# Two attention heads at a time: each product with v in one piece, three score buffers of two banks and two single banks, and a new hand-written order

## The chip, the cores and the metric

The kernel runs on one core of a Trainium2 chip. The metric is the device time of one execution in microseconds (us).

## What is computed

Four batches of eight heads attend over 576 tokens with 64 features per head. A score more than tau below its row's maximum is dropped before the softmax. The result goes through a top-2 mixture of eight experts and then through a dense two-layer network.

```python
scores = scale * np.matmul(q, k.transpose(0, 1, 3, 2))          # q, k, v: (4, 8, 576, 64)
thresh = np.max(scores, axis=-1, keepdims=True) - tau
scores = np.where(scores >= thresh, scores, -1000000000.0)
scores = scores - np.max(scores, axis=-1, keepdims=True)
attn = np.exp(scores)
attn = attn / (np.sum(attn, axis=-1, keepdims=True) + 1e-09)
x = np.matmul(attn, v)                                          # then to (2304, 512)
...
for e in range(8):                                              # two experts for each token
    h = np.maximum(x[mask] @ w1[e], 0.0)
    out[mask] += top2_w[mask, k, None] * (h @ w2[e])
...
g = np.where(h > 0.0, h, np.exp(np.minimum(h, 0.0)) - 1.0)      # h = x @ w_in
return g @ w_out
```

## The kernel before

The change lies in the attention, the first 300 us or so. The experts and the dense network behind it are the same code in both kernels.

Heads are taken in 16 pairs. The 2 x 576 queries of a pair make nine units: eight of 128 queries of one head (1 to 8), and unit 0, which holds the last 64 queries of both heads. A unit goes through these steps, which the order names by a letter, a unit and, behind the point, how many pairs it lags behind the newest one:

- `S` (`scores`, L247): four matmuls of 288 columns (eight for unit 0) into two banks of PSUM, a "wide" buffer.
- `R` (`rowmax`, L256), `H` (`thresh`, L260): VectorE reads the buffer for the row maximum and makes the threshold.
- `E` (`expo`, L265): ScalarE reads the buffer and writes the exponentials to SBUF.
- `M` (`mask`, L281): VectorE reads the buffer again, compares with the threshold, multiplies with the exponentials and writes P and its row sums. With that the wide buffer is free.
- `T` (`trans`, L169): four transpositions of P on TensorE into one bank, a "narrow" buffer; `A` (`evac_trans`, L312 and L315): ScalarE copies them to SBUF (`pt`), and the bank is free.

For each half of a pair's queries (half 0 has units 0 to 4, that is 320 columns, half 1 has units 5 to 8, 256 columns) follow `t` and `a` (the last 64 keys' part is transposed and copied to `ptt`, L328 and L332), `p` and `q` (the product with v, L352, and its copy to `ot`, L354), and `f` and `g` (`fin`, L378 and L382: the output is multiplied with a matrix that turns it to token rows and adds the gate's logits; ScalarE copies it to `ftmp`, L404, and GpSimd scales it, L403). Each of `T`, `t`, `p` and `f` needs a narrow bank: 15 of them for a pair.

A product with v has 64 output rows for each of the two heads, so it uses half of TensorE's columns for each head (128x64 in the profile's rows). It is in float32, which the profile shows as two MATMULs for one product: four blocks of 128 keys for two heads are 16 MATMULs, and the last keys (`ptt`) 4 more. Before, each product comes in two parts, `pa` (two blocks) and `pb` (two blocks and the last keys), with other work between, and holds its bank throughout.

PSUM has eight banks. Before, two wide buffers take four and four narrow ones the rest; in the first cycle a third wide buffer stands in for two of the narrow ones.

TensorE, ScalarE and VectorE run in exactly the order in which the code emits: `FIRST`, then `CYCLE` for each pair, then `REST`. GpSimd and the DMA queues are ordered by the framework. `G` and `F` in the order advance the routing of finished tokens to experts, a generator (`gate`), by one step; it comes at two places of the attention, late in it. `X` in `REST` prepares the first expert.

Of the kernel before, what the change touches and what calls it, by code (L numbers as in the profile page):

```python
# [9 lines left out]
F32 = mybir.dt.float32  # L10
# [15 lines left out]
def fused_kernel(ctx, tc, q, k, v, tau, w_gate, noise, wm, wf, out):  # L26
# [4 lines left out]
    NB = S // 128  # L31
# [90 lines left out]
    wide = [psum.tile([128, 2, 512], F32, name=f"bank{i}", bufs=1) for i in (2, 4)]  # L122
    fstack = ExitStack()
    third = fstack.enter_context(tc.tile_pool(name="fill", bufs=1, space=PSUM)).tile([128, 2, 512], F32, name="bank6")
    wide.append(third)

    def filled():

        wide[:] = [x for x in wide if x is not third]
        fstack.close()  # L130
        more = astack.enter_context(tc.tile_pool(name="bpsum", bufs=1, space=PSUM, reuse_waits="tile"))
        narrow[:0] = [more.tile([128, 512], F32, name=f"bank{i}", bufs=1) for i in (6, 7)]
# [184 lines left out]
    def tails(P, half):  # L317

        ps = mi(512)
# [6 lines left out]
        def out():  # L326
            t = PTT[P, half] = apool.tile([128, CW[half]], F32, name=f"ptt{half}", bufs=1)
# [9 lines left out]
    def pv(P, ch, part):  # L337

        vr, vt = VS[P]
        if P not in OT:  # L340
            OT[P] = apool.tile([128, S], F32, name="ot")
        n = CW[ch]
        if part == "a":
            PV_[P, ch] = mi(512)
        ps = PV_[P, ch][:, :n]
        for kb in (range(2) if part == "a" else range(2, NB + 1)):
# [7 lines left out]
        return lambda: act.activation(OT[P][:, o:o + n], ps, AF.Copy)  # L354

    PV_ = {}
# [8 lines left out]
    def fin(P, half):  # L365
# [8 lines left out]
        ps = mi(512)  # L374
# [13 lines left out]
        def post():  # L388
# [6 lines left out]
            if not half:  # L395
                x = tmp[:, 4 * NX:n].rearrange("p (i n) -> p i n", i=1)
                r = slice(b % 2 * 64, b % 2 * 64 + 64)
                for z in range(2):
                    f = slice(z * 64, z * 64 + 64)
                    todo += [(XT[b // 2][r, 2 * j + z:2 * j + z + 1], x[f, :, :D], rinv[f, 2 * NB:]),  # L400
                             (lgh[r, tt:tt + 1, :, 2 * j + z], x[f, :, D:], rinv[f, 2 * NB:])]
            for o, x, ri in todo:
                pool.tensor_tensor(o, x, ri[(slice(None),) * len(ri.shape) + (None,)].to_broadcast(list(x.shape)), op=OP.mult)  # L403
        return lambda: act.activation(tmp[:, :n], ps[:, :n], AF.Copy), post  # L404
# [162 lines left out]
    pool.memset(PTB[0][:, S:], 0.0)  # L567
    dve.memset(wx, 0.0)
# [4 lines left out]
    for s in range(2):  # L573
# [19 lines left out]
        S3.0 S4.0 S8.0 R3.0 E3.0 H3.0 M3.0 R4.0 R8.0 E4.0 H4.0 M4.0 S2.0 H8.0 S1.0 T3.0 E8.0 R2.0 M8.0 E2.0 A3.0 R1.0  # L593
        T4.0 S5.0 H2.0 A4.0 H1.0 E1.0 M2.0 R5.0 H5.0 M1.0 T2.0 E5.0 A2.0 S6.0 R6.0 T1.0 M5.0 S0.0 A1.0 E6.0 R0.0 T5.0
# [658 lines left out]
```

## Time and profile before

| | |
|---|---|
| median of 3 runs | 1210.14 us (1208.78 to 1210.71) |
| the profiled execution | 1208.14 us, of which its span is 1206.3 us |
| TensorE busy | 1165.9 us (97%) |
| VectorE busy | 717.5 us (59%) |
| ScalarE busy | 591.4 us (49%) |
| GpSimd busy | 275.6 us (23%) |
| share of TensorE in the chain that ended last | 87% |
| mean granted clock of TensorE | 0.991 |
| first matmul of the experts | 307.58 us after the span's start |

The span runs from the first to the last instruction; 1.84 us lie around it. "Busy" is the time in which an engine had an instruction under way. For TensorE the profile keeps two rows: PE for the matmuls, whose ends are modelled, and PEld for the loads of their stationary operands, which run ahead of the matmuls; so start-to-start times are the ones to add up.

### The profile page before, as it was taken

The numbers are of one execution on the slowest core, as the hardware profiler recorded it, in microseconds if no ns is written. First come the engines' busy times: TensorE is split into PE (matmuls) and PEld (weight loads), VectorE is DVE, ScalarE is ACT, GpSimd is POOL, SyncE is SP. The second block draws the span as 40 slices with busy tenths as digits, with TensorE's granted clock in tenths as the row PEclk, the third lists the DMA queues.
The fourth block names the chain that finished last, engine by engine and source line by source line (L and its number), as shares of the span: only waits on it lengthen the run. The fifth ranks groups of instructions, "written<-read, shape, count | busy, mean of one in ns | idle before, by whom it ended". The sixth has DMA issues, their size and how long they took to land.

```text
span 1206.3 us, 20167 instructions
## 1 busy us (share of the span) xinstructions
PE 1165.9 (97%) x7488; PEld 1012.3 (84%) x7488; DVE 717.5 (59%) x1560; ACT 591.4 (49%) x1201; POOL 275.6 (23%) x425
## 2 busy tenths in 40 slices
PE   5999999999899999999999999999999999999997
PEld 4777776776689999998999989788999999999996
DVE  6888889888756875656565657274333333333332
ACT  4777777777443433333333332175555444444443
POOL 6544465855520110000000102220111000000000
PEclk8999999999999999999999999899999999999999
DMA  7877765661596775555555435361122011010000
GB/s 203 245 199 228 215 183 142 204 176 71 176 343 218 246 236 167 187 158 202 158 180 157 166 128 170 123 254 52 53 88 71 10 62 53 2 52 19 1 18 20
DMA packets 66057, 169.96 MB, mean 141 GB/s; under 512 B 11424, under 2 KB 11552, under 8 KB 60320
## 3 DMA queue, kind: packets, MB, share of 16 engines
q1 hardware_dynamic: 54784, 138.94, 37.2%
q0 software_dynamic: 5760, 18.88, 4.6%
q10 hardware_dynamic: 5408, 10.78, 2.6%
q8 instruction: 61, 1.00, 0.3%
q14 instruction: 44, 0.36, 0.1%
HBM read 98.21 MB, written 43.52 MB: 117 GB/s over the span
## 4 chain that ended last, share of the span: by engine, by line
PE 87%; DVE 6%; DMA 3%; issue 2%; ACT 1%; POOL 1%; SPq 0%; ACTq 0%; DVEq 0%; POOLq 0%
PE h L834 17%; PE y L850 17%; PE h L1024 17%; PE o L1043 17%; PE bank L247 7%; PE bank L352 6%; PE bank L169 3%; DVE nmax L256 2%; PE h L169 1%; DMA wf_d<-c 1%; DVE P L281 1%; PE bank L378 1%; DMA w<-in_moe_dram 1%; DMA yg<-ys_d,yslot 1%; ACT e L265 0%
## 5 line engine op out<-in xcount | busy, mean ns | idle before, releaser
L1032 DVE SCALAR_TENSOR_TENSOR g<-fr,h 128x256 f32<-128x256 f32 x144 | 60.4, 420 | 172.5 <-ACT fr L1031 172.4
L265 ACT ACTIVATE e<-bank,nmax 128x576 f32<-128x576 f32 x144 | 105.8, 742 | 71.5 <-DVE nmax L256 66.6
L837 ACT ACTIVATE hh<-h 128x320 fp32r<-128x320 f32 (+2 forms) x128 | 55.4, 433 | 151.8 <-PE h L834 148.4
L818 POOL TENSOR_TENSOR c<-c,c 128x512 int32<-128x512 int32 x32 | 41.5, 1296 | 366.0 <-DVE c L817 366.0
L247 PE MATMUL bank<-kT,qT 128*128 128x288 f32 x320 | 105.3, 345 | 20.4 <-DVE P L281 10.3
L256 DVE TENSOR_REDUCE nmax<-bank 128x1 f32<-128x576 f32 x144 | 106.9, 750 | 26.0 <-PE bank L247 20.2
L1030 ACT ACTIVATE fr<-h 128x256 f32<-128x256 f32 x144 | 54.9, 381 | 119.5 <-PE h L1024 119.5
L281 DVE SCALAR_TENSOR_TENSOR P<-bank,thr,e 128x576 f32<-128x576 f32 x128 | 101.1, 815 | 13.1 <-ACT e L265 10.0
L247 PEld LDWEIGHTS bank<-kT,qT 128*128 128x128 f32 x320 | 62.2, 194 | 50.5 <-DVE P L281 31.2
L1034 DVE TENSOR_TENSOR gl<-g,gh 128x256 fp32r<-128x256 f32 x144 | 61.0, 426 | 67.3 <-ACT gh L1033 64.9
L747 POOL DMA_INDIRECT yg<-ys_d,yslot x36 | 38.5, 1071 | 267.9 <-PE h L169 169.4
L838 DVE SCALAR_TENSOR_TENSOR hl<-h,hh 128x320 fp32r<-128x320 f32 (+2 forms) x128 | 62.4, 487 | 61.5 <-ACT hh L837 61.0
L247 PE MATMUL bank<-kT,qL 128*128 128x288 f32 x320 | 92.0, 303 | 0.6 <-DVE qL L204 0.6
L1033 ACT ACTIVATE gh<-g 128x256 fp32r<-128x256 f32 x144 | 59.8, 416 | 62.5 <-DVE g L1032 62.5
L352 PE MATMUL bank<-pt,vr 128*64 128x256 f32 (+1 forms) x512 | 76.4, 419 | 0.0
L312 ACT ACTIVATE pt<-bank 128x512 f32<-128x512 f32 x128 | 71.4, 599 | 4.2 <-PE bank L169 3.6
L169 PE MATMUL bank<-ident,P_r 128*128 128x128 f32 x576 | 63.1, 247 | 3.1 <-DVE P L281 2.3
L169 PEld LDWEIGHTS bank<-ident,P_r 128*128 128x128 f32 x576 | 58.2, 142 | 9.1 <-issue 6.2
L247 PEld LDWEIGHTS bank<-kT,qL 128*128 128x128 f32 x320 | 62.9, 197 | 0.9 <-DVE qL L204 0.9
L1031 ACT ACTIVATE fr<-fr 128x256 f32<-128x256 f32 x144 | 59.9, 417 | 4.0
L352 PEld LDWEIGHTS bank<-pt,vr 128*64 128x64 f32 x512 | 31.8, 136 | 20.1 <-issue 3.6
L834 PE MATMUL h<-xh,w20h 128*128 128x320 f32 (+2 forms) x120 | 38.9, 324 | 0.0
(358 smaller groups left out, 3556.7 us busy)
## 6 DMA issues: line engine op xcount, KB each, us to landing
w<-in_moe_dram SPq DMA_DIRECT2D x36, 1024.0 KB
cr<-in_ffn_dram SPq DMA_DIRECT2D x32, 512.0 KB
xs_d<-t ACTq DMA_DIRECT2D x8, 1280.0 KB
ys_d<-y SPq DMA_DIRECT2D x40, 256.0 KB
xr<-xs_d SPq DMA_DIRECT2D x38, 256.0 KB
qT<-qh SPq DMA_DIRECT2D x60, 144.0 KB
wf_d<-c SPq DMA_DIRECT2D x32, 256.0 KB
w<-wf_d SPq DMA_DIRECT2D x8, 1024.0 KB
```

Of the source, the lines that this page charges most:

```text
L169: pe.matmul(o.bitcast(dt), x.bitcast(dt), ident.bitcast(dt), is_transpose=True, **{"start": True, "stop": True, **kw})
L247: pe.matmul(ps[:, hv, :S // 2], x[:, qc:qc + 128], kx[:, kc:kc + S // 2], start=(m == 0), stop=(m == n - 1))
L256: dve.tensor_reduce(ST[g][0], view(g), axis=AX.XY, op=OP.max, negate=True)
L265: act.activation(e, view(g), AF.Exp, bias=ST[g][0])
L281: dve.scalar_tensor_tensor(o.rearrange("p (a c) -> p a c", a=2), view(g), ST[g][1], E_.pop(g), op0=OP.is_ge, op1=OP.mult, accum_out=SU[P][ ...
L312: act.activation(turned_p(P, s, i // 2)[:, :, c:c + 128], ps, AF.Copy)
L352: pe.matmul(ps[s * 64:s * 64 + 64], lhs, rhs, start=(kb == 0), stop=(kb == NB))
L834: pe.matmul(ps[:, :step], w[:, c, f * 128:(f + 1) * 128], x[:, c, o:o + step], start=(m == 0), stop=(m == 3 * NC1 - 1))
L838: dve.scalar_tensor_tensor(hl[:, o:o + step], ps[:, :step], 0.0, f32(hh[:, o:o + step]), op0=OP.max, op1=OP.subtract)
L850: pe.matmul(Y[t], h[:, t * 128:(t + 1) * 128], w[:, f], start=(first and m == 0), stop=(last and m == 2))
L1024: pe.matmul(ps, w[:, c, f * 128:(f + 1) * 128], x[:, c], start=(m == 0), stop=(m == 3 * NC1 - 1))
L1043: pe.matmul(O[i], h[:, i * 128:(i + 1) * 128], w[:, f], start=(un == f == m == 0), stop=(un == NU2 - 1 and f == UF - 1 and m == 2))
```

## The change

- Each product with v is one step `p` of 16 + 4 MATMULs; a half's bank is held for that stretch alone.
- In `fin` the last 64 tokens of the two heads were two products of 64 output rows each, on half of the columns each. Now each of the two is a product over 128 tokens on all columns, 80 wide, into places of its own beside each other; of each, half of the rows is used. For that `ot` is wider by 64 columns of zeros and has two fixed buffers.
- Three wide buffers and two narrow ones throughout. `mi` no longer takes the narrow buffers in turn but the next one that nobody holds (`taken`).
- A new order. Half 0's product with v and both `fin` steps now lag two pairs behind, so the first cycle of `CYCLE` has none of them and `REST` has them for two pairs. The extra list `SECOND` goes.

```diff
-    wide = [psum.tile([128, 2, 512], F32, name=f"bank{i}", bufs=1) for i in (2, 4)]
...
-        narrow[:0] = [more.tile([128, 512], F32, name=f"bank{i}", bufs=1) for i in (6, 7)]
+    wide = [psum.tile([128, 2, 512], F32, name=f"bank{i}", bufs=1) for i in (2, 4, 6)]
...
-    def mi(*sh):
-        x = slot_of(narrow)[:, :math.prod(sh)]
+    taken = {}
+
+    def mi(key, *sh):
+
+        x = next(x for x in narrow if not any(x is y for y in taken.values()))
+        narrow[:] = [y for y in narrow if y is not x] + [x]
+        if key:
+            taken[key] = x
+        x = x[:, :math.prod(sh)]
...
-    def pv(P, ch, part):
+    def pv(P, ch):
...
-            OT[P] = apool.tile([128, S], F32, name="ot")
+            OT[P] = OTS[P % 2]
         n = CW[ch]
-        if part == "a":
-            PV_[P, ch] = mi(512)
-        ps = PV_[P, ch][:, :n]
-        for kb in (range(2) if part == "a" else range(2, NB + 1)):
+        ps = mi(("p", P, ch), 512)[:, :n]
+        for kb in range(NB + 1):
...
-            for s in range(2):
-                pe.matmul(ps[s * 64:s * 64 + 64, n:n + NX], OT[P][:, MAIN:S], wx[:, j, s], start=True, stop=True)
-            n += NX
+            for s, c in enumerate((MAIN, MAIN - 64)):
+                pe.matmul(ps[:, n:n + NX], OT[P][:, c:c + 128], wx[:, j, s], start=True, stop=True)
+                n += NX
...
-        E7.1 E8.1 H8.1 a0.1 M7.1 G.0 S1.0 M8.1 W.1 T6.1 G.0 R1.0 S2.0 R2.0 H1.0 G.0 H2.0 g1.2 E1.0 E2.0 T5.1 G.0 p0b.1
...
+        T0.1 M6.1 M5.1 S3.0 S1.0 G.0 A0.1 R8.1 E8.1 R3.0 G.0 T1.1 p0.2 H8.1 A1.1 G.0 R1.0 H1.0 E3.0 M8.1 G.0 H3.0 E1.0
+        F.0 t0.1 W.2 S4.0 G.0 q0.2 M3.0 T2.1 a0.1 G.0 R4.0 T5.1 S0.0 A2.1 G.0 A5.1 M1.0 H4.0 R0.0 G.0 t1.1 E4.0 T6.1
...
```

In the middle of the attention TensorE's order is the following, before, from the second MATMUL pair of a first part of half 1 (L352; 64x256 is what one product writes) over a score product (L247) and two transpositions (L169) to the end of the second part:

```order
L352 MATMUL bank_323<-pt_488,vr 64x256
L247 MATMUL bank_144<-kT,qT_156 128x288
L247 MATMUL bank_144<-kT,qL_158 128x288
L247 MATMUL bank_144<-kT,qT_156 128x288
L247 MATMUL bank_144<-kT,qL_158 128x288
L169 MATMUL bank_324<-ident,P_r 128x128 x4
L169 MATMUL bank_142<-ident,P_r 128x128 x4
L352 MATMUL bank_323<-pt_364,vr 64x256
L352 MATMUL bank_323<-pt_488,vr 64x256
L352 MATMUL bank_323<-pt_364,vr 64x256
L352 MATMUL bank_323<-pt_488,vr 64x256
L352 MATMUL bank_323<-ptt_478,vt_161 64x256 x2
```

And after the change, for the same half of the same pair (L348 is the line of the product with v now), with the transpositions ahead of and behind it:

```order
L165 MATMUL bank_141<-ident,P_r 128x128 x4
L348 MATMUL bank_142<-pt_455,vr 64x256
L348 MATMUL bank_142<-pt_322,vr 64x256
L348 MATMUL bank_142<-pt_455,vr 64x256
L348 MATMUL bank_142<-pt_322,vr 64x256
L348 MATMUL bank_142<-pt_455,vr 64x256
L348 MATMUL bank_142<-pt_322,vr 64x256
L348 MATMUL bank_142<-pt_455,vr 64x256
L348 MATMUL bank_142<-pt_322,vr 64x256
L348 MATMUL bank_142<-ptt_475,vt_158 64x256 x2
L165 MATMUL bank_141<-ident,P_r 128x128 x4
```

The score product and the two transpositions between the parts stand elsewhere in the cycle, and the two banks 141 and 142 take turns between transpositions and product.

Around `fin` of half 0 TensorE has before (transpositions into three narrow banks, then `fin`, L378 and L382, then the score product that takes the buffer 143):

```order
L169 MATMUL bank_324<-ident,P_r 128x128 x2
L169 MATMUL bank_142<-ident,P_r 128x128 x4
L169 MATMUL bank_141<-ident,P_r 128x128 x4
L378 MATMUL bank_323<-wx,ot 128x160 x2
L382 MATMUL bank_323<-wx,ot 64x80 x2
L247 MATMUL bank_143<-kT,qT_151 128x288
L247 MATMUL bank_143<-kT,qL_153 128x288
L247 MATMUL bank_143<-kT,qT_151 128x288
L247 MATMUL bank_143<-kT,qL_153 128x288
```

After, with both `fin` steps (L377, and L381 in place of L382) behind one another:

```order
L243 MATMUL bank_144<-kT,qT_148 128x288
L243 MATMUL bank_144<-kT,qL_150 128x288
L243 MATMUL bank_144<-kT,qT_148 128x288
L243 MATMUL bank_144<-kT,qL_150 128x288
L377 MATMUL bank_142<-wx,ot_167 128x160 x2
L377 MATMUL bank_141<-wx,ot_167 128x160 x2
L381 MATMUL bank_141<-wx,ot_167 128x80 x2
L165 MATMUL bank_142<-ident,P_r 128x128 x4
```

The last tokens' products have 128 rows in place of 64, a score product stands ahead of the two `fin` steps, and a transposition behind them.

ScalarE's order shows how the narrow banks come free. Before, around the copy of a half's product (L354; L312 and L315 copy transpositions, L265 is an exponential, L404 copies `fin`):

```order
L265 ACTIVATE e<-bank_143,nmax 128x576
L265 ACTIVATE e<-bank_144,nmax 128x576
L312 ACTIVATE pt_1179<-bank_324 128x4x128
L312 ACTIVATE pt_1179<-bank_142 128x4x128
L354 ACTIVATE ot<-bank_323 128x320
L265 ACTIVATE e<-bank_143,nmax 128x576
L265 ACTIVATE e<-bank_144,nmax 128x576
L328 ACTIVATE ptt_1206<-bank_141 128x256
L312 ACTIVATE pt_1216<-bank_323 128x4x128
```

After, around the copy of half 0's product (L353), where the copies L326, L330 and L309 empty the banks of the steps `t`, `T2` and `T5` in turn (L261 is an exponential):

```order
L353 ACTIVATE ot_167<-bank_142 128x320
L326 ACTIVATE ptt_1135<-bank_141 128x256
L330 ACTIVATE ptt_1135<-bank_141 64x64 x2
L309 ACTIVATE pt_1070<-bank_142 128x4x128
L309 ACTIVATE pt_1155<-bank_141 128x4x128
L261 ACTIVATE e<-bank_145,nmax 128x576
```

Before, a copy is followed by others from three more narrow banks; now bank 141 and bank 142 alternate, and each copy stands between TensorE's steps of one before and one after.

## Rows read from the trace of the kernel before

**Rows 1.** Page, part 4: the chain that ended last, by engine

```profile
PE 87%; DVE 6%; DMA 3%; issue 2%; ACT 1%; POOL 1%; SPq 0%; ACTq 0%; DVEq 0%; POOLq 0%
```

**Rows 2.** Timeline of TensorE, first `fin` products of L382: first, tenth and last cycle

```profile
36.98 0.36 PE L382 MATMUL bank<-wx,ot 128*64 128x80 f32 x4
...
193.25 0.36 PE L382 MATMUL bank<-wx,ot 128*64 128x80 f32 x4
...
303.27 0.36 PE L382 MATMUL bank<-wx,ot 128*64 128x80 f32 x4
```

**Rows 3.** Busy time by stretch: length, each engine busy, granted clock, DMA

```profile
54.32:71.67 17.35, 17.11 (x135) 13.06 (x135) 15.07 (x39) 13.45 (x28) 9.33 (x19) 1.00 0.78 221
...
195.00:212.00 17.00, 15.40 (x125) 11.34 (x125) 15.80 (x64) 11.85 (x26) 10.21 (x26) 1.00 0.50 127
```

**Rows 4.** Waits from 20 to 300 us: total, times, longest

```profile
PEld bank L247 <- DVE P L281: 29.6, 55, 1.6
...
DVE nmax L256 <- PE bank L247: 18.8, 52, 2.2
...
ACT e L265 <- DVE nmax L256: 59.5, 90, 3.1
```

**Rows 5.** Timeline, half 1's product in two parts; start, duration

```profile
109.70 1.08 PE L352 MATMUL bank<-pt,vr 128*64 128x256 f32 x8
...
110.72 0.40 PE L247 MATMUL bank<-kT,qT 128*128 128x288 f32 x1
...
112.09 1.08 PE L352 MATMUL bank<-pt,vr 128*64 128x256 f32 x8
...
113.01 0.60 PE L352 MATMUL bank<-ptt,vt 128*64 128x256 f32 x4
...
113.54 0.40 PE L247 MATMUL bank<-kT,qT 128*128 128x288 f32 x1
```

**Rows 6.** Timeline of the last pair, where both parts follow one another

```profile
303.46 2.04 PE L352 MATMUL bank<-pt,vr 128*64 128x256 f32 x16
...
305.19 0.75 PE L352 MATMUL bank<-ptt,vt 128*64 128x256 f32 x4
...
305.86 0.88 PE L169 MATMUL bank<-ident,t 128*128 128x128 f32 x8
```

**Rows 7.** Timeline around `fin` of half 0

```profile
105.69 0.78 PE L378 MATMUL bank<-wx,ot 128*128 128x160 f32 x4
...
106.39 0.20 PEld L382 LDWEIGHTS bank<-wx,ot 128*64 128x64 f32 x4 [0.17 <-issue]
...
106.97 0.40 PE L247 MATMUL bank<-kT,qT 128*128 128x288 f32 x1 [0.22 <-DVE P L281]
...
107.34 0.29 PE L247 MATMUL bank<-kT,qT 128*128 128x288 f32 x1
```

**Rows 8.** Timeline, one transposition and ScalarE's copies out of narrow banks

```profile
113.05 0.59 ACT L312 ACTIVATE pt<-bank 128x512 f32<-128x512 f32 x1
...
114.17 0.46 PE L169 MATMUL bank<-ident,PT_r 128*128 128x128 f32 x4
...
116.76 0.38 ACT L328 ACTIVATE ptt<-bank 128x256 f32<-128x256 f32 x1
...
117.02 0.44 ACT L332 ACTIVATE ptt<-bank 64x64 f32<-64x64 f32 x2
...
121.49 0.45 ACT L354 ACTIVATE ot<-bank 128x320 f32<-128x320 f32 x1
```

**Rows 9.** Timeline, start of the second and of the last cycle, and the experts

```profile
47.83 0.40 PE L247 MATMUL bank<-kT,qT 128*128 128x288 f32 x1
...
298.49 0.87 PE L169 MATMUL bank<-ident,P_r 128*128 128x128 f32 x8
...
308.41 3.01 PE L834 MATMUL h<-xb 128*128 128x256 f32 x23 [0.45 <-DVE xb L695]
```

**Rows 10.** Timeline, TensorE's longest wait in the first expert

```profile
320.19 0.73 PE L850 MATMUL y<-w01h,hl 128*128 128x512 f32 x1 [3.91 <-DVE hl L838]
```

More of the change, by code (lines that the diff above doesn't have):

```diff
@@ L121, in fused_kernel @@
     narrow = [psum.tile([128, 512], F32, name=f"bank{i}", bufs=1) for i in range(2)]
-    wide = [psum.tile([128, 2, 512], F32, name=f"bank{i}", bufs=1) for i in (2, 4)]
[L123 to L131, printed above, removed]
-        narrow[:0] = [more.tile([128, 512], F32, name=f"bank{i}", bufs=1) for i in (6, 7)]
+    wide = [psum.tile([128, 2, 512], F32, name=f"bank{i}", bufs=1) for i in (2, 4, 6)]
     def slot_of(slots):
@@ L308, in evac_trans @@
         ps = PS_.pop(g)
+        taken.pop(("T", g))
         if u:
@@ L317, in tails @@
     def tails(P, half):
-        ps = mi(512)
+        ps = mi(("t", P, half), 512)
         for n in range(2):
@@ L326, in out @@
         def out():
+            taken.pop(("t", P, half))
             t = PTT[P, half] = apool.tile([128, CW[half]], F32, name=f"ptt{half}", bufs=1)
@@ L353, in pv, with out @@
         o = OC[ch]
-        return lambda: act.activation(OT[P][:, o:o + n], ps, AF.Copy)
-    PV_ = {}
+        def out():
+            taken.pop(("p", P, ch))
+            act.activation(OT[P][:, o:o + n], ps, AF.Copy)
+        return out
     G2, NX = 2 * E, D + 2 * E
@@ L373, in fin @@
                 XT[b // 2] = xpool.tile([128, H, D], F32, name="xt", bufs=2)
-        ps = mi(512)
+        ps = mi(("f", P, half), 512)
         n = 4 * NX
@@ L399, in post, with out @@
                     f = slice(z * 64, z * 64 + 64)
[L400 to L401 removed]
+                    todo += [(XT[b // 2][r, 2 * j + z:2 * j + z + 1], x[f, z:z + 1, :D], rinv[f, 2 * NB:]),
+                             (lgh[r, tt:tt + 1, :, 2 * j + z], x[f, z:z + 1, D:], rinv[f, 2 * NB:])]
             for o, x, ri in todo:
                 pool.tensor_tensor(o, x, ri[(slice(None),) * len(ri.shape) + (None,)].to_broadcast(list(x.shape)), op=OP.mult)
[L404 removed]
+        def out():
+            taken.pop(("f", P, half))
+            act.activation(tmp[:, :n], ps[:, :n], AF.Copy)
+        return out, post
     SC, SCN = [], set()
@@ L567, in fused_kernel @@
     pool.memset(PTB[0][:, S:], 0.0)
+    OTS = [apool.tile([128, S + 64], F32, name=f"ot{i}", bufs=1) for i in range(2)]
+    for t in OTS:
+        pool.memset(t[:, S:], 0.0)
     dve.memset(wx, 0.0)
@@ L614, in run @@
         elif x == "p":
-            AFTER["p" + g[0], P] = pv(P, int(g[0]), g[1])
+            AFTER[what, P] = pv(P, int(g))
         elif x == "f":
@@ L704, in fused_kernel @@
             u = 0
-            for x in REST if c == NP else SECOND + CYCLE if c == 1 else CYCLE if c else FIRST:
+            for x in REST if c == NP else CYCLE if c else FIRST:
                 what, lag = x.split(".")
@@ L718, in fused_kernel @@
                     next(first, 0)
-                if c == 0 and what == "S6":
-                    filled()
                 if what[0] == ("p" if c == NP and u else "M"):
```

30 lines of the change are left out of this document (14 added, 16 removed).

## The prediction

> **What bounds the kernel now.** I read the page first: TensorE makes 87% of the chain that ended last [rows 1]. So the question is where TensorE's time in the attention goes, since nothing else is edited. The timeline of TensorE gives the beat: the `fin` product of L382 comes once in a cycle, at 36.98 in the first and at 193.25 nine cycles later, which is 17.36 us for one, and at 303.27 in the last [rows 2]. The last six take 110.02 us in place of 104.2: 5.9 us more, in the cycles in which the routing's steps run beside the attention.
>
> The table by stretch shows what a cycle is made of: TensorE 17.11 of 17.35 us, VectorE 15.07, ScalarE 13.45 [rows 3]. TensorE is the bound, with VectorE 13% behind. The list of waits says how TensorE and VectorE are tied: its loads of `kT` and `qT` waited 55 times, 29.6 us in all, for a mask (L281), that is for a wide buffer to come free, some 3.5 times in a cycle for 0.54 us. VectorE waited 52 times for score products, and ScalarE 90 times for a row maximum, 59.5 us in all [rows 4]. These are the waits of a loop through two wide buffers: a buffer is filled, reduced, exponentiated, masked, and only then filled again.
>
> **The change part by part, for one cycle.**
>
> *(a) Each product in one piece.* Half 1's product takes 1.02 us for its first part (109.70 to 110.72) and 1.45 for its second (112.09 to 113.54), 2.47 together [rows 5]. In the last pair the two parts already stand behind one another: 16 MATMULs take 1.73 us (303.46 to 305.19) and the last four 0.67 up to the next transposition [rows 6], or 0.53 up to a score product [rows 5]: 2.40 or 2.26. So one piece saves 0.07 to 0.21 us. A transposition follows it now, but I do not know how much of the 0.67 is that; I take 0.15, and as much for half 0, since what is saved is a second entry and exit and not columns: 0.3, bounds 0.14 and 0.42.
>
> *(b) The last tokens' products over all columns.* Four MATMULs of 160 columns on the whole array take 0.70 us (105.69 to 106.39). Those of L382, 80 wide on half of the columns, take 0.58, of which 0.22 are a wait for a mask: 0.36 [rows 7]. Four of 80 columns on the whole array are half of 0.70, 0.35: nothing lost. The Trainium skill speaks against this edit: by "TensorE: Matmul & The Clock Gate", Part 3, products in different column tiles run at the same time, so putting two such products on the whole array makes them follow one another. By that rule the 0.36 would double, 5.8 us more over 16 pairs; the row of 160 columns says otherwise, and I go by the row. What the edit and the new place of `fin` can give is the 0.22 wait at the score product behind it, since a transposition stands there now and the mask has a third buffer's time: 0.2, bounds 0 and 0.22.
>
> *(c) Three wide buffers.* A matmul whose load could not run ahead shows 0.40 us, the ones behind it 0.29 [rows 7]. With a third buffer the mask that frees a buffer lies a whole unit of VectorE's work further back (15.07 us for nine units, 1.7 us [rows 3]), so loads can run ahead again. Of the 3.5 such waits in a cycle one is counted in (b); 2.5 times 0.11 are 0.25, bounds 0 and 0.4.
>
> *(d) Two narrow banks in place of four.* This is the price. All 15 fills of a cycle now alternate between two banks, so a fill starts only when ScalarE has emptied the one before the last. A transposition has its result after 0.46 us, and the copy takes 0.59 [rows 8]: 1.05 us in which one bank is bound, while TensorE makes something of about that length between two uses of a bank almost everywhere (a score product is 0.63, 113.54 to 114.17 [rows 5, 8]; a product with v over 2). The tightest place that I find is behind half 0's product. There TensorE goes on with `t`, `S4` and `T2`, 0.63 and twice 0.3 to 0.46, 1.2 to 1.5 us, and then wants for `T5` the bank of `t`. ScalarE must first copy the product (0.45) and then the two pieces of `ptt` (0.38 and 0.44): 1.27 us, and it starts some 0.1 late because the last matmul has to end. So TensorE waits 0 to 0.25 there; I take 0.15 as the whole loss of (d). What would wait behind `T5` is `S0`, 1.2 us long, and then VectorE. The bound above is in the rivals.
>
> *(e) VectorE* keeps its instructions. It has 15.07 us of work, and in the cycles with routing it got 15.80 done in 17.00 [rows 3], 93%; at that density 15.07 need 16.2 us, under what I come to. So it need not be the new bound.
>
> *(f) First and last cycle.* The first cycle of the new order lacks half 0's product and both `fin`s, and `REST` has them twice. That work is half 0's product, 2.40 us times 320/256 at most, 3.0, and `fin`, 0.70 twice and 0.35: 4.7 us. Now the second cycle starts at 47.83 and the experts' first products run from 308.41, 9.9 us after the last cycle's start at 298.49 [rows 9]. The new second cycle should start earlier by that work and more, since it starts at another point of the pair (fewer masks are behind it), and the new `REST` is longer by the same. I take nothing for the balance, bounds 4 us either way: for, a fill in which VectorE hardly stops; against, `REST` has its products, copies and `fin`s one behind the other through two banks.
>
> *(g) Routing and hand-over.* The 5.9 us of the cycles with routing and the waits at the first expert, the longest 3.91 us [rows 10], have the same instructions behind them. I take no change, bounds 3 us.
>
> **The sum.** 0.3 + 0.2 + 0.25 - 0.15 = 0.6 us a cycle, 16.75 in place of 17.36, and 16 pairs: 9.6 us. The profiled execution took 1208.14 us (its span 1206.3 and 1.84 around it), so 1198.5. The median of the runs lies 2.0 above that execution, and I predict **1199**, between 1198.5 and 1200.5. The bounds of (a) to (d) alone are 0 and 1.0 us a cycle.
>
> **Rivals.**
>
> *VectorE sets the beat.* If the new order leaves VectorE at a density of 88%, hardly more than its 87% now, a cycle is 17.1 us and the gain 0.25 x 16 = 4 us: 1204. For: its waits for score products, 18.8 us [rows 4], are only moved when TensorE reaches a buffer earlier. Against: 93% with routing [rows 3], and three buffers let two reductions wait ahead of it.
>
> *Nothing is gained.* Parts (b) and (c) may be waits hidden behind VectorE anyway; then 0.14 of (a) against 0.15 of (d) leave 1208.
>
> *The narrow banks stop TensorE: slower.* ScalarE works in order, and a copy that stands behind an exponential waits with it for a row maximum, 0.66 us on average [rows 4]. If in each cycle two of the 15 fills meet such a copy, TensorE loses 1.32 us and wins 0.75: 0.57 x 16 = 9 us more, 1217. It turns at 0.75 us a cycle. For: with four banks a late copy costs nothing, with two it stops the second fill behind it. Against: six of the fifteen copies stand right behind an exponential, and where I followed them (the copies of `fin`, of half 1's product, of `T7`) a product of 0.6 us or more stands on TensorE before the bank is wanted.
>
> *All of it is given back.* The loader stops for 0.17 us where the array goes over to half of its columns [rows 7]. The new order has two such stretches in a cycle in place of five, each with a way in and a way out: six changes fewer at 0.17 are 1.0 us, and with no loss in (d) 16 us: 1192. The Trainium skill, "TensorEngine Tiling (Array Packing)", Key Properties, says that a change of the tiling mode drains TensorE; by that rule, which the 0.17 bears out in part, this would be the outcome.
>
> **How the numbers follow.** Forecast 0.58 (1194 to 1203), VectorE's beat 0.15, nothing 0.08, banks 0.11, all given back 0.08. The range 1191 to 1208 leaves out the banks, half of "nothing" and a little of the last. A change of 0.2% is about what can be told: the three runs span 0.16%. Faster by more than that are the first, second and last case, 0.81; within it 0.08; slower 0.11.
>
> **What would show it.** In the new trace: products of L348 of 16 MATMULs in about 1.75 us and cycles of 16.6 to 16.9 us between the `fin`s of L381 (a, b); few waits of L243 for masks (c); waits of transpositions for ScalarE below 0.3 us a cycle, at `T5` if anywhere (d); VectorE above 89% busy (e); the experts' first products near 298 (f). I am wrong if transpositions wait for copies by 0.75 us a cycle, if VectorE stays at 15.07 in 17.1 or more, or if a cycle is shorter but the experts do not start earlier.

## The result, and the profile after

The changed kernel takes 1197.59 us (median of 5 runs, 1194.82 to 1199.38), the one before on the same chip 1208.78 (5 runs): the ratio is 0.9914, with a 95% interval of 0.9899 to 0.9929, so it is 0.86% faster. The forecast of 1199 us lies 1.4 above the median. The profiled execution took 1198.59 us, its span is 1196.8 in place of 1206.3, its mean granted clock 0.995.

The timeline of TensorE gives the beat again, now by L381, which is L382 of before [rows 2]. Shown are the products of the first, second, ninth, tenth, thirteenth, fourteenth and last pair (pairs are counted from 1 here).

```profile
53.73 0.55 PE L381 MATMUL bank<-wx,ot 128*128 128x80 f32 x2
...
70.26 0.57 PE L381 MATMUL bank<-wx,ot 128*128 128x80 f32 x4
...
183.38 0.57 PE L381 MATMUL bank<-wx,ot 128*128 128x80 f32 x4
...
205.77 0.57 PE L381 MATMUL bank<-wx,ot 128*128 128x80 f32 x4
...
254.18 0.57 PE L381 MATMUL bank<-wx,ot 128*128 128x80 f32 x4
...
273.70 0.57 PE L381 MATMUL bank<-wx,ot 128*128 128x80 f32 x4
...
293.42 0.57 PE L381 MATMUL bank<-wx,ot 128*128 128x80 f32 x4
```

A cycle without routing is 16.16 us (seven of them from 70.26 to 183.38), 1.20 less than before and not 0.6. But the first product comes 16.75 us later than it did, the two cycles with routing take 22.39 and 19.52, and the last two come 19.7 us after the fourteenth (273.70 to 293.42), because the last part of the order holds what the cycles put off. So an account has to go from the first instruction to the experts.

The busy time by stretch (length, then PE, PEld, DVE, ACT, POOL, clock, DMA), for a plain cycle and the two with routing; it answers to [rows 3].

```profile
70.26:86.42 16.16, 16.16 (x136) 13.45 (x135) 14.81 (x39) 13.76 (x28) 7.94 (x16) 1.00 0.77 221
183.38:205.77 22.39, 17.76 (x147) 13.98 (x146) 19.53 (x80) 14.48 (x30) 14.42 (x32) 1.00 0.50 135
254.18:273.70 19.52, 17.60 (x142) 13.88 (x141) 17.90 (x67) 14.61 (x30) 9.36 (x25) 1.00 0.11 41
```

In the plain cycle TensorE has no idle time left, and its work has shrunk from 17.11 to 16.16. VectorE is at 92%, with 1.3 us of reserve in place of 2.3.

The list of waits from 20 to 300 us (total, times, longest), as in [rows 4].

```profile
ACT e L261 <- DVE P L277: 12.8, 26, 2.7
...
ACT e L261 <- DVE nmax L252: 7.3, 15, 2.2
...
PEld bank L243 <- DVE P L277: 4.3, 8, 1.2
```

The loads behind a mask waited 8 times in place of 55, and ScalarE waited 7.3 us for a row maximum in place of 59.5: the loop through the wide buffers is no longer tight. What ScalarE waits for now is its own exponentials' buffers, which a mask has to free.

The timeline of TensorE in one plain cycle (the score products left out) shows both products with v and both `fin`s.

```profile
105.81 1.95 PE L348 MATMUL bank<-pt,vr 128*64 128x256 f32 x16
107.59 0.60 PE L348 MATMUL bank<-ptt,vt 128*64 128x256 f32 x4
108.12 0.54 PE L165 MATMUL bank<-ident,P_r 128*128 128x128 f32 x4
...
110.91 2.37 PE L348 MATMUL bank<-pt,vr 128*64 128x320 f32 x16
113.11 0.71 PE L348 MATMUL bank<-ptt,vt 128*64 128x320 f32 x4
113.75 0.36 PE L165 MATMUL bank<-ident,P_r 128*128 128x128 f32 x2
...
117.66 1.25 PE L377 MATMUL bank<-wx,ot 128*128 128x160 f32 x8
118.74 0.57 PE L381 MATMUL bank<-wx,ot 128*128 128x80 f32 x4
119.11 0.52 PE L165 MATMUL bank<-ident,P_r 128*128 128x128 f32 x4
```

Half 1's product takes 2.31 us from start to start (105.81 to 108.12), 0.16 less than its two parts [rows 5]. The last tokens' products take 0.37 (118.74 to 119.11) against 0.36 [rows 7], and the 0.22 behind them is gone. And a gain that the prediction did not see: the `fin`s of both halves now stand side by side, and their eight products take 1.08 us (117.66 to 118.74), where four took 0.70 [rows 7] and the other four 0.71: about 0.33 less a pair. Whether standing side by side is the reason, a run below tells: it is not.

Where the time went back: TensorE's waits in the fill, in the cycles with routing, and at the first expert (the longest there was 3.91 us before [rows 10]; now it is 1.30 at that line, and 2.91 at 315.13 for the last of the routing).

```profile
40.79 0.37 PE L243 MATMUL bank<-kT,qT 128*128 128x288 f32 x1 [0.88 <-DMA kT<-kl]
...
51.44 2.50 PE L377 MATMUL bank<-wx,ot 128*128 128x160 f32 x8 [2.21 <-ACT ptt L326]
...
191.35 0.51 PE L165 MATMUL bank<-ident,P_r 128*128 128x128 f32 x4 [2.00 <-DVE gm L482]
...
205.13 0.81 PE L377 MATMUL bank<-wx,ot 128*128 128x160 f32 x4 [0.91 <-DVE over L530]
...
273.05 0.81 PE L377 MATMUL bank<-wx,ot 128*128 128x160 f32 x4 [1.11 <-DVE over L550]
...
300.13 4.51 PE L836 MATMUL h<-xb 128*128 128x256 f32 x23 [0.34 <-DVE xb L699]
...
309.23 0.50 PE L852 MATMUL y<-w01h,hl 128*128 128x512 f32 x1 [1.30 <-DVE hl L840]
```

Behind the wait of 2.21 us TensorE's granted clock is 0.50, the lower level of 1.2 GHz, from 51.4 to 53.7: the eight products at 51.44 take 2.29 us (51.44 to 53.73) where they take 1.08 in a plain cycle. And the experts' first 23 products take 4.51 us in place of 3.01 [rows 9]; the granted clock there is 0.62 (300.0 to 304.5).

For an account of the span the marks must enclose the same steps. Both `fin`s lag two pairs now, so the product of one pair stands in the cycle in which that of the next pair stood before: 53.73 answers to the second product before, and 273.70 to the fifteenth.

```profile
54.32 0.36 PE L382 MATMUL bank<-wx,ot 128*64 128x80 f32 x4
...
286.03 0.36 PE L382 MATMUL bank<-wx,ot 128*64 128x80 f32 x4
```

With these, 193.25 [rows 2] and 308.41 [rows 9] the account is:

| stretch | before | after | difference |
|---|---|---|---|
| start to the first mark | 54.32 | 53.73 | -0.6 |
| eight cycles without routing | 138.93 | 129.65 | -9.3 |
| five cycles with routing among them | 92.78 | 90.32 | -2.5 |
| from there to the experts' products | 22.38 | 26.43 | +4.1 |
| experts' products to the end | 897.9 | 896.7 | -1.2 |
| span | 1206.3 | 1196.8 | -9.5 |

Thirteen times 1.20 are 15.6. The five cycles with routing won 2.5 in place of 6.0, so 3.5 were given back there; the eight others won 9.3 in place of 9.6. The fill and the drain of the attention, the first and the fourth line, cost 3.5 together.

### The profile page after: what moved, and what is told of

The parts are those of the page before. It is cut to its first block, busy times and chain, and to the rows that moved or that the text cites. A ratio compares the mean times of both kernels' runs of the same rounds, so it can differ in the third digit from the quotient of the medians.

```text
span 1196.8 us, 20094 instructions
## 1 busy us (share of the span) xinstructions
PE 1152.9 (96%) x7488; PEld 1018.3 (85%) x7488; DVE 711.6 (59%) x1560; ACT 596.1 (50%) x1201; POOL 273.2 (23%) x427
## 4 chain that ended last, share of the span: by engine, by line
PE 85%; DVE 5%; DMA 4%; ACT 1%; POOL 1%; issue 1%; SPq 0%; ACTq 0%; DVEq 0%; POOLq 0%
PE h L1026 17%; PE o L1045 17%; PE h L836 16%; PE y L852 16%; PE bank L348 6%; PE bank L243 6%; PE bank L165 4%; PE h L165 1%; PE bank L377 1%; DVE P L277 1%; DMA wf_d<-c 1%; DMA w<-in_moe_dram 1%; DMA kT<-kl 1%; DMA yg<-ys_d,yslot 1%; PE bank L381 1%
## 5 line engine op out<-in xcount | busy, mean ns | idle before, releaser
L261 ACT ACTIVATE e<-bank,nmax 128x576 f32<-128x576 f32 x144 | 104.8, 740 | 29.0 <-DVE nmax L252 14.7
L243 PE MATMUL bank<-kT,qT 128*128 128x288 f32 x320 | 101.3, 334 | 16.1 <-DVE kT L192 8.2
L243 PE MATMUL bank<-kT,qL 128*128 128x288 f32 x320 | 91.2, 302 | 0.0
L309 ACT ACTIVATE pt<-bank 128x512 f32<-128x512 f32 x128 | 75.1, 598 | 19.0 <-PE bank L165 16.7
L243 PEld LDWEIGHTS bank<-kT,qT 128*128 128x128 f32 x320 | 62.1, 194 | 20.0 <-DVE kT L192 8.2
L165 PEld LDWEIGHTS bank<-ident,P_r 128*128 128x128 f32 x576 | 61.9, 142 | 19.8 <-issue 8.2
L165 PE MATMUL bank<-ident,P_r 128*128 128x128 f32 x576 | 69.7, 246 | 5.4 <-DVE gm L482 2.0
L348 PE MATMUL bank<-pt,vr 128*64 128x320 f32 (+1 forms) x512 | 69.1, 412 | 0.4 <-ACT pt L312 0.4
L243 PEld LDWEIGHTS bank<-kT,qL 128*128 128x128 f32 x320 | 62.6, 196 | 0.0
L348 PEld LDWEIGHTS bank<-pt,vr 128*64 128x64 f32 x512 | 33.9, 136 | 21.7 <-ACT pt L312 0.6
L785 ACT ACTIVATE xh<-h 128x512 fp32r<-128x512 f32 x38 | 22.4, 589 | 34.5 <-PE h L165 34.5
```

The source lines that it names most:

```text
L165: pe.matmul(o.bitcast(dt), x.bitcast(dt), ident.bitcast(dt), is_transpose=True, **{"start": True, "stop": True, **kw})
L243: pe.matmul(ps[:, hv, :S // 2], x[:, qc:qc + 128], kx[:, kc:kc + S // 2], start=(m == 0), stop=(m == n - 1))
L261: act.activation(e, view(g), AF.Exp, bias=ST[g][0])
L309: act.activation(turned_p(P, s, i // 2)[:, :, c:c + 128], ps, AF.Copy)
L348: pe.matmul(ps[s * 64:s * 64 + 64], lhs, rhs, start=(kb == 0), stop=(kb == NB))
```

## The experiments

The ratio of each is to runs of the kernel before on the same chip, whose median was between 1207.99 and 1212.25 us, so ratios are compared and not times. The changed kernel's is 0.9914 (0.9899 to 0.9929). "Cycle" is the distance between two products of the last tokens, away from the routing. Of a line of the order only the part with the change is shown.

### One part alone, in the kernel before

**Each product in one piece, at the place of its second part.** In the order the `p0a`, `p1a` go, and `p0b`, `p1b` make the whole:

```diff
-        for kb in (range(2) if part == "a" else range(2, NB + 1)):
+        for kb in range(NB + 1):
```

> The kernel before, with each product with v in one piece, at the place of its second part; banks and order are otherwise those of before. Theory (a second way into and out of a product with v costs 0.15 us a time, as the new trace shows: 2.31 for 2.47 and 2.84 for 2.99): 0.31 us a pair, 4.7 us over 15 cycles if TensorE is the bound at both places, so 3 to 5 us faster. Rival, each change of the array's mode costs 0.17 us: two stretches fewer a pair, four changes, 0.68 us a pair, 10 us faster. Rival, it is the third wide buffer alone: no change.

Measured: 1231.1 us, ratio 1.0188 (1.0166 to 1.0209): slower, against all three expectations. A cycle is 18.92 us. Busy time of one, and the waits in it:

```profile
93.52:112.45 18.93, 17.05 (x136) 13.26 (x135) 15.07 (x39) 13.58 (x28) 7.94 (x17) 1.00 0.72 197
```

```profile
PEld bank L247 <- DVE P L281: 3.4, 5, 1.2
DVE nmax L256 <- PE bank L247: 2.7, 3, 1.3
```

TensorE and VectorE wait for one another. The reading of these waits: while TensorE is on a product of 2.3 to 2.8 us, VectorE has at most two filled buffers, runs out of them, and then TensorE stands before buffers that aren't free. The 0.15 a product is real in the rows of the changed kernel, but it wasn't to be had at this place: between the parts stood the work that gave VectorE its next scores.

**The same, near the place of the first part** (half 0 behind `S1`, half 1 in front of `S6`):

```diff
-        E7.1 E8.1 H8.1 a0.1 M7.1 G.0 S1.0 M8.1 W.1 T6.1
+        E7.1 E8.1 H8.1 a0.1 M7.1 G.0 S1.0 p0.1 M8.1 W.1 T6.1
-        H5.0 G.0 T1.0 E5.0 T3.0 g0.1 G.0 M5.0 S0.0 R0.0 p1a.1 G.0
+        H5.0 G.0 T1.0 E5.0 T3.0 g0.1 G.0 M5.0 S0.0 R0.0 p1.1 G.0
```

> The kernel before with each product with v in one piece, now near the place of its first part: half 0's behind S1 at the start of the cycle, half 1's in front of S6. Banks and the rest of the order are those of before. Theory, a product of 2.3 to 2.8 us in one piece keeps TensorE from the scores while two wide buffers give VectorE nothing else to do: a loss at this place too, 0.5 to 1.6 us a cycle, 8 to 24 us slower than before. Rival, only the place was wrong in the run with the products at the place of the second part: 0.31 us a pair, 4 to 5 us faster than before.

Measured: 1276.71 us, ratio 1.0567 (1.0544 to 1.0591), a cycle of 21.0 to 22.7 us with TensorE busy for 17.31 of 21.40. So it was not only the place: the loss is there at both, and larger than expected here.

**The last tokens' products over all columns**, with zeros behind `ot`:

```diff
-            for s in range(2):
-                pe.matmul(ps[s * 64:s * 64 + 64, n:n + NX], OT[P][:, MAIN:S], wx[:, j, s], start=True, stop=True)
-            n += NX
+            for s, c in enumerate((MAIN, MAIN - 64)):
+                pe.matmul(ps[:, n:n + NX], OT[P][:, c:c + 128], wx[:, j, s], start=True, stop=True)
+                n += NX
```

> The kernel before, with the last tokens' products with the weights over all columns (padded with zeros), everything else as before. Theory: the four products take 0.36 us either way and the 0.22 us behind them are a wait for a mask that stays: no change, within 0.1%. Rival, products in different column tiles ran side by side: 0.36 us more a pair, 5.8 us slower. Rival, each change of the array's mode costs 0.17 us: one stretch less a pair, two changes, 5 us faster.

Measured: 1209.91 us, ratio 1.0005 (0.9993 to 1.0018), a cycle of 17.38 us. No change, as in the theory, but by two effects that cancel: the four products of L378 take 0.62 us in this run (107.13 to 107.75) in place of 0.70, since no product on half of the columns follows them, and the last tokens' products with the wait behind them 0.64 (107.75 to 108.39) in place of 0.58. The run that takes this part back, below, shows the same without the wait.

**The old order with the new banks** (three wide, two narrow) and products in one piece; `A6`, `g1`, `g0`, `A2` and `A4` stand some steps earlier, so that no three of the narrow banks' contents live at once:

```diff
-        M8.1 W.1 T6.1 G.0 R1.0 S2.0 R2.0 H1.0 G.0 H2.0 g1.2 E1.0 E2.0 T5.1 G.0 p0b.1
+        M8.1 W.1 g1.2 T6.1 G.0 R1.0 S2.0 R2.0 H1.0 G.0 H2.0 E1.0 E2.0 A6.1 T5.1 G.0 p0.1
...
-        T2.0 R6.0 G.0 E0.0 T4.0 p1b.1 H0.0 G.0 H6.0 E6.0 A4.0
+        T2.0 R6.0 G.0 E0.0 A2.0 T4.0 A4.0 p1.1 H0.0 G.0 H6.0 E6.0
```

> The order of before, with each product with v in one piece, and with three wide buffers and two narrow banks throughout; eight copies and hand-overs stand a few steps earlier, as far as two narrow banks demand it. Theory, the third wide buffer by itself gives 0.25 to 0.3 us a cycle: 0.31 and 0.3 a pair, 8 to 10 us faster than before, and 4 to 5 faster than the products in one piece alone. Rival, the new order is what makes two narrow banks bearable: transpositions wait for copies by 0.5 us a cycle and more, and it is no faster than the products in one piece alone, or slower than before.

Measured: 1312.09 us, ratio 1.0856 (1.0831 to 1.0881), cycles of 23.9 us. The waits of one of them, from 161.40 to 185.31:

```profile
PE bank L348 <- ACT pt L309: 2.8, 2, 1.9
PEld bank L165 <- ACT ptt L326: 1.8, 1, 1.8
PE bank L165 <- ACT ptt L326: 1.6, 1, 1.6
```

TensorE stands before narrow banks whose copy is behind an exponential on ScalarE; its mean granted clock in that stretch is 0.93. This is the forecast's slower rival, "the narrow banks stop TensorE", and well above the 0.57 us a cycle that it was priced at. Two narrow banks are free of cost in a plain cycle of the new order and ruinous in this one.

### One part taken back, in the changed kernel

**The last tokens' products on half of the columns again** (the diff above, reversed).

> The changed kernel, with the last tokens' products again on half of the columns, two and two. Theory: 0.36 us either way, no change within 0.1%. Rival, each change of the array's mode costs 0.17 us: 2.7 to 5.4 us slower.

Measured: 1199.85 us, ratio 0.994 (0.9922 to 0.9959), a cycle of 16.17 and the same span of 1196.8 us in the profile. The interval overlaps with that of the changed kernel; the cycle says that the form of these products is worth nothing. Its rows say why:

```profile
115.50 1.25 PE L377 MATMUL bank<-wx,ot 128*128 128x160 f32 x8
116.68 0.36 PE L381 MATMUL bank<-wx,ot 128*64 128x80 f32 x4
116.97 0.54 PE L165 MATMUL bank<-ident,P_r 128*128 128x128 f32 x4
```

The four products on half of the columns take 0.29 us (116.68 to 116.97) in place of 0.37 over all columns (118.74 to 119.11 in the changed kernel): two of them, one for each half of the columns, start within 0.01 us of each other. But the eight products ahead of them take 1.18 (115.50 to 116.68) in place of 1.08, since the last of them stands 0.23 us before the next in place of 0.14: going over to half of the columns costs 0.09, about what the two halves win.

**The products in two pieces again**, with four transpositions between them:

```diff
-        G.0 T1.1 p0.2 H8.1 A1.1 G.0
+        G.0 p0a.2 T1.1 p0b.2 H8.1 A1.1 G.0
-        G.0 A7.0 p1.1 E5.0 H5.0 G.0 q1.1 T4.0 A4.0 S8.0 G.0
+        G.0 A7.0 p1a.1 E5.0 H5.0 G.0 T4.0 p1b.1 q1.1 A4.0 S8.0 G.0
```

> The changed kernel, with each product with v in two pieces again (key blocks 0 and 1, and the rest), with a group of four transpositions between them. Theory: the second way in and out costs 0.15 us a time, 0.3 us a pair, 16 pairs, 4 to 5 us slower than the changed kernel's 1197.6. Rival, it was the buffers and the order that gave all: no change.

Measured: 1218.5 us, ratio 1.0055 (1.0043 to 1.0067), a cycle of 17.61 us. The timeline of half 1's and half 0's product in a cycle:

```profile
126.83 0.50 PE L165 MATMUL bank<-ident,P_r 128*128 128x128 f32 x4 [0.80 <-DVE thr L256]
127.26 1.08 PE L350 MATMUL bank<-pt,vr 128*64 128x256 f32 x8
...
130.86 1.30 PE L350 MATMUL bank<-pt,vr 128*64 128x320 f32 x8
132.09 0.53 PE L165 MATMUL bank<-ident,P_r 128*128 128x128 f32 x4
132.55 1.30 PE L350 MATMUL bank<-pt,vr 128*64 128x320 f32 x8
133.68 0.71 PE L350 MATMUL bank<-ptt,vt 128*64 128x320 f32 x4
134.32 0.36 PE L165 MATMUL bank<-ident,P_r 128*128 128x128 f32 x2
```

Half 0's pieces take 1.23 and 1.77 us, 3.00 against 2.84: the 0.16 of a second way in and out, as expected. The cycle lost 1.45, however: TensorE waits 0.80 us for the narrow bank of the transposition that now stands between half 1's pieces (named is a threshold, which was long done; the copy of `T7` out of that bank runs from 125.89 to 126.5, behind two exponentials), and works for 16.80 in place of 16.16. So this run gives a size for one piece, on half 0, and shows what one bank too early costs; it is not the price of the pieces alone.

**The `fin`s apart**, with `S7` between them:

```diff
-        t1.1 E4.0 T6.1 M4.0 G.0 S7.0 a1.1 f1.2 R7.0 A6.1
+        t1.1 E4.0 T6.1 a1.1 f1.2 M4.0 G.0 S7.0 R7.0 A6.1
```

> The changed kernel, with the products with the weights of the two halves apart again: a score product (S7) stands between them, and nothing else is moved on TensorE. Theory: side by side they took 1.08 us, apart 0.70 and 0.71; 0.33 us a pair, 16 pairs, 5 us slower than 1197.6. Rival, the 0.33 us are waits that the third wide buffer removed: no change, within 0.1%.

Measured: 1208.0 us, ratio 0.9969 (0.9952 to 0.9986), a cycle of 16.69 us:

```profile
102.60:119.29 16.69, 16.52 (x136) 13.49 (x135) 14.97 (x39) 13.72 (x27) 7.92 (x16) 1.00 0.78 218
```

TensorE works 0.36 us longer, as expected, but not where it was expected:

```profile
117.58 0.81 PE L377 MATMUL bank<-wx,ot 128*128 128x160 f32 x4
118.11 0.40 PE L243 MATMUL bank<-kT,qT 128*128 128x288 f32 x1
...
118.75 0.71 PE L377 MATMUL bank<-wx,ot 128*128 128x160 f32 x4
119.29 0.57 PE L381 MATMUL bank<-wx,ot 128*128 128x80 f32 x4
```

Apart, the four products take 0.53 us (117.58 to 118.11) and 0.54 (118.75 to 119.29), 1.07 together, no more than the 1.08 side by side. So standing side by side is worth nothing, and the 0.33 us come from what stands ahead of them and behind them (below). What the cycle lost lies elsewhere: 0.30 us between the six transpositions ahead of the first `fin` and its first product (0.77 from start to start, where these transpositions take 0.47 in the changed kernel; 0.17 of it is a wait, now that it stands nearer to the copy that frees its bank), and 0.23 at the score products. The whole loss, 0.0055 of 1208 or 6.6 us, fits 0.53 us a cycle.

**One more reduction on VectorE** in each cycle, its result unused:

```diff
+        if g % NU == 4:
+            dve.tensor_reduce(apool.tile([128, 1], F32, name="more", bufs=4), view(g), axis=AX.XY, op=OP.max)
```

> The changed kernel with one more reduction on VectorE in each cycle (the maximum of unit 4 a second time, 0.74 us, its result unused). VectorE then has 15.6 us of work in a cycle of 16.16. Theory, TensorE is the bound and VectorE has 1.3 us of reserve, of which 0.74 are to be had: 0 to 0.25 us a cycle, 0 to 4 us slower than 1197.6. Rival, VectorE's idle time is waits that it can't fill, and it sets the beat already: 0.74 us a cycle, 11 to 12 us slower.

Measured: 1201.92 us, ratio 0.9949 (0.9935 to 0.9963), a cycle of 16.51 us with 15.54 on VectorE. The 0.74 us cost 0.35: VectorE does not set the beat, but only half of what is added to it still hides.

### What gave time back

**The routing's sums in unused columns of a wide buffer**:

```diff
+    def spare(sh):
+        x = wide[0][:, 0, 320:320 + math.prod(sh[1:])]
+        return x.rearrange("p (a b) -> p a b", b=sh[-1]) if len(sh) > 2 else x
...
-            gates.append(gate(T0[x] if x > 1 else 0, T0[x + 1], lambda sh: mi(None, *sh[1:])))
+            gates.append(gate(T0[x] if x > 1 else 0, T0[x + 1], spare))
```

> The changed kernel, with the small sums of the routing (72 and 8 columns) in columns of a wide buffer that the scores don't use, so that no narrow bank waits for VectorE to read them. Theory: the waits of 0.47, 0.91 and 1.1 us of the two cycles with routing go, 2 to 2.5 us faster than 1197.6, and those cycles at 18.3 to 21.5 us in place of 19.5 and 22.4. Rival, TensorE then waits for a mask at the next place: no change. Rival, the sums wait for a mask of that buffer and VectorE waits for them: 1 to 2 us slower.

Measured: 1201.5 us, ratio 0.9918 (0.9904 to 0.9931): no change. The two cycles with routing are 21.05 and 18.54 us, 1.3 and 1.0 shorter, but the two behind the first of them take 17.28 and 17.25 in place of 16.11 and 16.15. The waits were passed on.

**The routing's maximum four steps later**:

```diff
-        yield from pause(4)
+        yield from pause(8)
```

> The changed kernel, with the routing's maximum on VectorE four steps of the order later, so that it doesn't wait for GpSimd ahead of the masks. Theory: the wait of 2.06 us of VectorE and the 2.0 us of TensorE behind it go, 2 us faster than 1197.6. Rival, the later steps of the routing then fall on other places that wait, and the gain is passed on: no change or up to 2 us slower.

Measured: 1198.56 us, ratio 0.9894 (0.9877 to 0.991), which overlaps with the changed kernel's. Two stretches of its profile:

```profile
181.77:200.91 19.14, 17.39 (x147) 13.88 (x146) 18.97 (x76) 14.85 (x30) 12.88 (x32) 1.00 0.57 141
200.91:218.02 17.11, 16.42 (x137) 13.54 (x136) 15.29 (x43) 12.85 (x25) 13.02 (x23) 1.00 0.67 199
```

The first cycle with routing shrinks from 22.39 to 19.14, and then VectorE works in 18.97 of it: with GpSimd out of the way VectorE is the bound there. The three cycles behind it take 17.11 to 17.78, though, and over five cycles only 0.6 us are won (89.68 for 90.32). Why these three are slow is not settled: TensorE works 0.2 to 0.6 us longer in each and has a longer wait in each, for a threshold of VectorE (0.62) in the first and for copies of ScalarE (0.46 and 1.40) in the others.

**The zeros two cycles later** (ScalarE issues eight transfers that clear the experts' input, one a cycle):

```diff
-        if u == 5 and 1 <= P <= E:
-            e = P - 1
+        if u == 5 and 3 <= P <= E + 2:
+            e = P - 3
```

> The changed kernel, with the eight transfers of zeros that ScalarE's queue issues one in a cycle started two cycles later (cycles 3 to 10 in place of 1 to 8). Theory: the copy behind the second of them no longer comes 1.1 to 2.7 us late, TensorE's stop at the product with the weights (0.7 to 2.2 us in the five traces of this order so far) goes, the first full cycle's product of the last tokens comes near 51 us in place of 53.7, and the kernel is 1 to 2 us faster than 1197.6 (against before: 0.990). Rival, what the transfer waited for holds up the next instruction as well: no change. Rival, the zeros collide with the loads of later cycles: up to 2 us slower.

Measured: 1196.45 us, ratio 0.9908 (0.9892 to 0.9924), which overlaps with the changed kernel's. In the changed kernel ScalarE stood in front of the second of these transfers:

```profile
50.40 0.56 ACTq L645 DMA_DIRECT2D xs_d<-t  x1
51.00 0.38 ACT L326 ACTIVATE ptt<-bank 128x256 f32<-128x256 f32 x1 [2.66 <-DMA qL<-ql]
```

With the zeros later TensorE has no wait between 36 and 56 us, and pair 1's product comes at 50.73, 3.0 us earlier, as expected: the stop of 2.21 is gone and the low clock behind it. (The stop differs from one execution to another. In six other runs with this order, nearly unchanged, and the zeros where they were, that product comes at 51.6 to 52.7, so against those 0.8 to 2.0 us are won and not 3.0.) But the experts start only 1.75 earlier (298.38). The stretch in which it was lost:

```profile
180.02:204.08 24.06, 20.31 (x147) 15.70 (x146) 19.13 (x80) 14.62 (x30) 16.17 (x33) 0.86 0.66 196
...
184.00:188.00 4.00, 2.59 (x26) 1.66 (x23) 2.53 (x21) 1.89 (x5) 2.08 (x6) 1.00 0.49 112
...
190.00:192.00 2.00, 2.00 (x11) 1.98 (x10) 1.93 (x7) 0.20 (x1) 0.88 (x2) 0.50 0.93 225
...
198.00:200.00 2.00, 2.00 (x19) 1.95 (x19) 1.93 (x8) 1.40 (x5) 1.66 (x2) 1.00 0.63 158
```

The first row is the whole cycle with routing, the others stretches of it. TensorE was busy for 2.59 of the 4 us ahead, with a wait of 1.41 us for VectorE; then its granted clock is 0.50, the lower level of 1.2 GHz, for the 6 us or so around 192, and 1.00 again behind them. The 147 matmuls of this cycle take 20.31 us where the changed kernel's 147 take 17.76: 2.55 more at the lower clock, of which TensorE's shorter waits give 0.88 back. So this cycle is 1.67 us longer than in the changed kernel (24.06 for 22.39), which is more than the 1.25 of the 3.0 us that did not arrive at the experts.

**Both**:

> The changed kernel with the zeros two cycles later and the routing's maximum four steps later, together. Theory: the two are independent, the first moves the start of the tenth cycle by 3 us (180.0 in place of 183.4 in the profile), the second keeps VectorE from stopping for GpSimd, which was 0.6 us over the five cycles with routing, and the experts begin near 297 us in place of 300.1: 2 to 4 us faster than the changed kernel, 0.987 to 0.989 of before. Rival, what is won ahead of the routing is lost in it, since its steps are set by GpSimd and by TensorE's clock there: 0.991, no better than the zeros alone.

Measured: 1194.76 us, ratio 0.9866 (0.9842 to 0.9889), whose interval lies below that of the changed kernel. Pair 1's product comes at 49.02, pair 14's at 267.93, and the experts' products at 294.99, 5.1 us earlier than in the changed kernel; the span is 2.9 shorter, so 2.2 are lost behind that point. It beats both kernels.

## Why the prediction came out

The time was right, 1199 for 1197.6, but by two errors that cancel, which is luck: the cycle saves twice what was forecast, and the routing, the fill and the drain, all taken at nothing, cost 7 us. The forecast was sixteen times 0.6, 9.6 us; it came to thirteen times 1.20, 15.6, less 7.3 (3.5 with routing, 3.5 in fill and drain, 0.3 in the first cycles), and 1.2 won behind the attention: 9.5.

- *(a) One piece* was sized right for this kernel: 0.16 and 0.15 (half 0: 2.84 for the 2.99 of its two parts). What the step did not see is that it isn't a part by itself. Alone it makes the kernel 1.9% or 5.7% slower; by the waits of the first of these runs, what stood between the two parts was the work in which two wide buffers got filled.
- *(b) The last tokens' products*: 0 for the form and 0.2 for the wait, and both came, the first by luck. The 0.35 was half of 0.70, but 0.16 of the 0.70 belong to the neighbours: without them four products of 160 columns take 0.54, half of that is 0.27, and four of 80 take 0.37. And the two halves of the columns do work at once, as the rule of the Trainium skill, "TensorE: Matmul & The Clock Gate", Part 3, has it, by which half-width products in different column tiles run at the same time: the trace agrees, 0.29 for 0.37. What hid it is the 0.09 us at the product ahead.
- *(c) Three wide buffers*: the waits of L243 for masks fell from 55 to 8, and the score products' busy time in a cycle is 7.05 us for 7.42, 0.37 against the 0.25 of the forecast. How much of it is the third buffer is not shown: in the new order no score product follows products on half of the columns any more, whose first matmul shows 0.40 us [rows 5] in place of the 0.37 behind transpositions, and no run has the third buffer without the two narrow banks. That the third buffer is the condition of (a) is likely for the same reason as above, and not shown either.
- *(d) Two narrow banks* were to cost 0.15 and cost nothing in a plain cycle: TensorE has no idle time there. The expected wait at `T5` does not appear. That they stop TensorE is a matter of the order, as the old order with the new banks shows.
- *Not in the sum*: 0.33 at the two `fin`s. It is not that they stand side by side (apart they take 1.07, with a score product between them). Before, each stood behind transpositions, where the second product starts 0.21 us after the first in place of 0.14, and ahead of products on half of the columns, where the last product takes 0.23 in place of 0.14: 0.16 each, twice. With it the parts are 0.31 + 0.22 + 0.33 + 0.37 = 1.23 for the measured 1.20.
- *(e) VectorE* is above 89% and not the bound, as said, at 14.85 of 16.16. But its reserve went from 2.3 to 1.3 us a cycle, and that was not carried on to (g).
- *(f) Fill and drain* cost 3.5, within the bound of 4: the drain is 4.1 us longer, near the 4.7 of work that moved there, but the fill is only 0.6 shorter. In it lie the stop behind the zeros and the one for `kT`, 3.1 us, and 1.2 us of low clock behind the first of them. That the new order brings a transfer on ScalarE's queue to a place where its wait is felt was not looked at.
- *(g) Routing and hand-over, "no change"*, is the step that failed: 3.5 us more in the cycles with routing, 1.2 less behind them. The same instructions stand in less cover. VectorE's extra work in the two long cycles is 4.7 and 3.1 us against a reserve of 1.3 in each, so 5.1 us do not fit; before, the extra work of the five cycles was 4.2, 1.6, 0.2, 0 and 1.6 us against 2.3 in each, so 1.9 did not. An estimate from that is 3.2 of the 3.5; no run isolates it. The trace shows the time as the wait for GpSimd (2.0) and those for the sums (0.91 and 1.11), but taking either away passes most of it on.

Of the rivals, "all of it is given back" ended nearest to the cycle (16.4 by its 1.0), and its reason, fewer changes of the array's mode, is borne out in part. By the Trainium skill, "TensorEngine Tiling (Array Packing)", Key Properties, a change of the mode drains TensorE; the trace agrees in that the change has a price, 0.09 us at the product ahead of a stretch on half of the columns, and a second stretch costs 0.16 by itself. For three stretches fewer that is three times 0.09 and, for the two of the products with v, 0.31, less the 0.08 that the last tokens' two halves won: an estimate of 0.5 of the 1.20. The rival's 0.17 was the loader's pause at one such change, not the time that TensorE loses.

## What to carry to other kernels

Parts of a change that share buffers and an order are not terms of a sum: tried without the new order, they made between no difference and 8.6% more, and with it 0.86% less. When a cycle gets shorter on the bound engine, look at once at what used to hide in the next engine's reserve: here its reserve fell from 2.3 to 1.3 us a cycle, and the cycles with other work gave 3.5 us back. And before a stretch of products is credited with a gain, look at what stands ahead of it and behind it: the same four products took 0.70 us between transpositions and products on half of the columns, and 0.54 between score products and products on all columns.

## What the runs showed of the hardware

Going over from all of TensorE's columns to half of them cost 0.09 us at the product ahead: from its start to that of the next product it was 0.23 us in place of 0.14. The two halves then worked at once, and four products of 80 columns took 0.29 us in place of 0.37. That the two cancel here, so that the form is worth nothing, was not expected, and neither was that four products cost 0.70 or 0.54 by their neighbours alone. Nor was the clock: waits of TensorE of 2.00 us in one kernel (191.35) and of 1.41 us in another, in the same cycle of the program, left the granted clock at 1.00 in the first and were followed by 0.50 in the second, for some 6 us; one of 2.21 us in the first kernel's fill was followed by 0.50 for some 3 us.
